# Cosine attention and a two-layer network: 112 or 128 weight columns in the attention's matmuls

## The chip, the cores and the metric

The kernel runs on one core of one Trainium2 chip. The metric is the device time in microseconds of one execution, from the first to the last instruction of the core and what lies around it. The core has an engine for matrix products (TensorE; in the profile PE for matmuls and PEld for the loads of their weights), VectorE (DVE), ScalarE (ACT), GpSimd (POOL), and SyncE (SP), which here only issues transfers. Each engine works through its own queue in order, and waits for the others by semaphores.

## The reference

Eight batches of 12 heads, each with 448 positions of 64 numbers. Queries and keys are brought to length one, the scores are divided by tau = 0.1, and a softmax over the keys weights the values:

```python
q_n = q / (np.linalg.norm(q, axis=-1, keepdims=True) + 1e-06)
k_n = k / (np.linalg.norm(k, axis=-1, keepdims=True) + 1e-06)
scores = np.matmul(q_n, k_n.transpose(0, 1, 3, 2)) / tau
attn = softmax(scores)                 # over the keys
attn_out = np.matmul(attn, v)          # (8, 12, 448, 64)
x = attn_out.transpose(0, 2, 1, 3).reshape(3584, 768)
h = x @ w_in                           # 768 -> 2048
out = (h / (1 + np.exp(-1.702 * h))) @ w_out   # 2048 -> 768
```

Inputs and output are FP32.

## The kernel before

**Tiles.** A unit of attention work is a pair of heads, called x (0 to 47; six to a batch). Its 448 positions are cut into C = 4 chunks of P = 112, which lie on 112 partitions. One load each brings q, k and v of a pair (`load`, L226). Squares and their sums give the norms (`square`, `reduce`, `norm_a`, `norm_b`; `root` and `inverse` for batch 0), `scale` (L310) writes normalised q and k in FP16 into the tile qks, with query (index 0) before key (index 1). For batches 0 and 1 the tile is transposed on TensorE (`transposes`, L333) and copied by DVE (`transposed`, L348), for the later ones by a DMA (`dma_transposed`, L352). Either way qkT holds, on 128 partitions, 64 numbers of the one head over 64 of the other, and along the free axis 448 query positions and 448 key positions.

**Scores.** For a chunk c of keys the 112 key columns are the weights, and the queries move: two matmuls, one for each head, each on 64 of the array's rows. `scores` (L363) takes all 448 queries, for batches 2 to 7; `scores_h` (L424) takes half of them, 224, and two chunks at once, for batches 0 and 1. The result sp has key positions on its partitions. `exp` (L375) makes one of the eight tiles et from it; such a tile has 2 × 448 columns and 64 more, which hold ones from the start (L770).

**Products with values.** The weights are columns of et, that is, query positions; 65 columns move: 64 of the values and a column of ones, which gives the softmax's denominator. `attend` (L388, batches 2 to 7) goes through the queries in four blocks of 128 columns, of which the last runs past the head's 448. `attend_h` (L440, batches 0 and 1, one half of the queries at a time) takes two blocks of 112 for each head, and sums over the four chunks of keys: 16 matmuls. `normalise` or `normalise_h` divides; the result is transposed by a DMA (`turn`, L414) or on TensorE (`turn_h`, L467), into xT.

**The network.** `mm1` (L490; `mm1_h` for batch 0, by halves) multiplies xT with w_in, `tanh` and `gate` apply the activation, `mm2` (L544) multiplies with w_out, `halve` and `store` bring the result out. The weights w_in and w_out are loaded in two halves each by POOL's queue (L582 and L588).

**Order.** The order of the work on every engine is fixed when the program is built. `Plan` (L35) holds every step with its engine, a price in us, a due time, the steps it follows (`after`), and the buffers that it takes and frees. `order` (L71) plays the steps through with those prices; whenever an engine is free, it takes the ready step with the earliest due time. For each change between matmuls on 64 and on 128 rows the price is 0.12 us. `emit` (L48) then emits the steps in that order; before a TensorE step that stands later than TensorE was free, for planned times up to 50 us, it puts fillers (`fill`, L345: a transpose of the identity into an unused part of PSUM). Steps of POOL and DVE that share a port are linked (`port`), so that a POOL step of that kind follows the last such DVE step in the planned order. Some loads are held until others have landed (`hold`): batch 1's loads for w_in, w_out for the last q load of batch 1 (L762), batch 2's first load and with it SP's queue behind it for the second half of w_out (L614).

Of the kernel before, what the change touches and what calls it, by code (L numbers as in the profile page):

```python
# [10 lines left out]
FP32 = mybir.dt.float32  # L11
# [23 lines left out]
class Plan:  # L35
# [6 lines left out]
    def add(self, name, eng, us, due, emit, after=(), takes=(), frees=(), dma=None, rows=128, hold=(), turn=False):  # L42
        after = list(after) + list(hold)
        if turn:
            self.turns.append((due, len(self.turns), name))
        self.ops[name] = (eng, us, due, emit, after, takes, frees, dma, rows, hold)
# [106 lines left out]
def kernel(  # L153
# [12 lines left out]
    B, H, S, D = q.shape  # L166
    NTOK, DM = out.shape
    DFF = moe_w_in.shape[1]
    P = 112
# [10 lines left out]
    SH = S // 2  # L180
# [26 lines left out]
    ps_s = psum("ps_s", 2)  # L207
# [16 lines left out]
    q32, k32, v32, sqs, n2s, nrms, rss, qkss, qkTs = [{} for _ in range(9)]  # L224
# [85 lines left out]
    def scale(x, ti, eng):  # L310
        if x not in qkss:
            qkss[x] = p_qks.tile([P, 2, C, 2, D], FP16, name="qks")
        src = (q32, k32)[ti].pop(x)
        return eng.tensor_tensor(  # L314
            out=qkss[x][:, ti].rearrange("p c j d -> p j c d"),
            in0=src,
            in1=rss[x][:, ti, :, :, None].to_broadcast((P, 2, C, D)),
            op=ALU.mult,
        )


    def values(x, c, e0, e1):
        return vts[x % NV][:, c].rearrange("p j e -> p (j e)")[:, e0:e1]
# [9 lines left out]
    def transposes(x):  # L333
        tps = tps0[:, : 2 * S].rearrange("p (t s) -> p t s", t=2)
        qks = qkss.pop(x)
        for ti in (1, 0):
            for c in range(C):
                nc.tensor.transpose(
                    out=tps[:, ti, c * P : (c + 1) * P],
                    in_=qks[:, ti, c].rearrange("p j d -> p (j d)"),  # L340
                    identity=ident[:P, :P],
                )
        tpss[x] = tps
# [16 lines left out]

    tpss, exps, sps, avps, xss = [{} for _ in range(5)]

    def scores(x, c):  # L363
        qkT = qkTs[x]
        sp = sps[x, c] = ps_s.tile([P, 2, 512], FP32, name="sp")
        for j in range(2):
            nc.tensor.matmul(  # L367
                out=sp[:, j, :S],
                lhsT=qkT[64 * j : 64 * (j + 1), 1, c * P : (c + 1) * P],
                rhs=qkT[64 * j : 64 * (j + 1), 0, :],  # L370
                start=True,
                stop=True,
            )

    def exp(*key):  # L375
        e = exps[key] = ets[len(exps) % NE]
        kw = dict(bias=ebias[:P]) if shift > 0 else {}
        nc.scalar.activation(  # L378
            out=e[:, : 2 * S].rearrange("p (j s) -> p j s", j=2),
            in_=sps.pop(key)[:, :, :S],  # L380
            func=AF.Exp,
            scale=inv_tau,
            **kw,
        )
# [37 lines left out]


    def scores_h(x, h, u):  # L424
        qkT = qkTs[x]
        sp = sps[x, h, u] = ps_s.tile([P, 2, 512], FP32, name="sp")
        for i in range(2):
            c = 2 * u + i
            for j in range(2):
                nc.tensor.matmul(  # L430
                    out=sp[:, j, i * SH : (i + 1) * SH],
                    lhsT=qkT[64 * j : 64 * (j + 1), 1, c * P : (c + 1) * P],
                    rhs=qkT[64 * j : 64 * (j + 1), 0, h * SH : (h + 1) * SH],
                    start=True,
                    stop=True,
                )
# [3 lines left out]
    def attend_h(x, h):  # L440
        ps = avps[x, h] = ps_m.tile([128, 512], FP32, name="mm")
        for i in range(2):
            for j in range(2):
                o = 132 * i + 65 * j
                for c in range(C):
                    at = j * S + (c % 2) * SH + i * P
                    nc.tensor.matmul(  # L447
                        out=ps[:P, o : o + D + 1],
                        lhsT=exps[x, h, c // 2][:, at : at + P],
                        rhs=values(x, c, D * j, D * j + D + 1),  # L450
                        start=(c == 0),
                        stop=(c == C - 1),
                    )
# [146 lines left out]
    add = plan.add  # L600
# [7 lines left out]
    def due_of(x):  # L608
        return x if x < HP else 2 * x

    for x in range(NPAIR):
        s, grp, first = due_of(x), group_of[x], x < HP
        early = due_of(grp[0]) - (4 if first else 8)
        hold = [("w_in", int(x >= HP + 3))] if HP <= x < 2 * HP else [("w_out", 1)] if x == 2 * HP else []  # L614
        for ti, nm in ((1, "k"), (0, "q")):
            add(("load", nm, x), "ACT" if x + ti == 0 else "SP", 0.5, s - 13, partial(load, x, (q32, k32)[ti], (q, k)[ti], nm + "32"),
                takes=[(nm, 1)], dma=PAIR, hold=hold, turn=True)
            pl = sq_pool(x, ti)
            add(("sq", ti, x), "POOL" if pl else "ACT", 1.0 if pl else 0.53, early + ti * 0.1, partial(square, x, ti),
                after=[("load", nm, x)], takes=[("sq", 1), ("port", int(pl))], frees=[("port", int(pl))])  # L620
            add(("red", ti, x), "DVE", 0.6, early + 0.2, partial(reduce, x, ti),
                after=[("sq", ti, x)], frees=[("sq", 1)])
            dve = x == 0 and ti == 0
            add(("scale", ti, x), "DVE" if dve else "POOL", 0.7 if dve else 1.0, early + 0.5 if first else s - 5 - ti * 0.1,
                partial(scale, x, ti, nc.vector if dve else nc.gpsimd),
                after=[("norm", 1, grp)], takes=[("qks", 1), ("port", 1)], frees=[(nm, 1), ("port", 1)])
# [6 lines left out]
        if x == grp[0] and not first:  # L633
# [6 lines left out]
            after=[("load", "v", x)], takes=[("vt", 1), ("port", 1 - ca)], frees=[("v", 1), ("port", 1 - ca)])  # L640
        if x < TURN:
            add(("tp", x), "PE", 0.4, s - 3, partial(transposes, x),
                after=[("scale", 0, x), ("scale", 1, x)], takes=[("a", 1), ("qkT", 1)], frees=[("qks", 2)])
            add(("qkT", x), "DVE", 0.6, s - 3, partial(transposed, x), after=[("tp", x)], frees=[("a", 1)])
        else:
            add(("qkT", x), "SP", 1.3, s - 3, partial(dma_transposed, x),
                after=[("scale", 0, x), ("scale", 1, x)], takes=[("qkT", 1)], frees=[("qks", 2)],
                dma=packets(2 * P, C * D * 4))
        if x < HALF:
            for h in range(2):  # L650
                sh = x + HP * h if first else s + h
                for u in range(2):
                    key = (x, h, u)
                    add(("s",) + key, "PE", 0.2, sh, partial(scores_h, *key), after=[("qkT", x)] + [("s", min(x + AHEAD, HP - 1), 0, 1)] * (first and h),
                        takes=[("sp", 1)], frees=[("qkT", h * u)], rows=64)
                    add(("exp",) + key, "ACT", 0.82, sh + 0.1, partial(exp, *key), after=[("s",) + key],
                        takes=[("exp", 1)], frees=[("sp", 1)])
                es = [("exp", x, h, u) for u in range(2)] + [("cast", x)]
                add(("at", x, h), "PE", 0.85, sh + 1, partial(attend_h, x, h), after=es,
                    takes=[("mm", 1)], frees=[("exp", 2), ("vt", h)])  # L660
                add(("nx", x, h), "DVE", 0.65, sh + 1, partial(normalise_h, x, h), after=[("at", x, h)],
                    takes=[("xs", 1)])
                add(("turn", x, h), "PE", 0.15, sh + 1, partial(turn_h, x, h), after=[("nx", x, h)],
                    frees=[("xs", 1)])
                add(("x", x, h), "ACT" if x in XA and not h else "DVE", 0.35, sh + 1, partial(turned_h, x, h), after=[("turn", x, h)],
                    takes=[("x", 1 - h)], frees=[("mm", 1)])
            continue
        for c in range(C):
            add(("s", x, c), "PE", 0.19, s + c // 2, partial(scores, x, c), after=[("qkT", x)],
                takes=[("sp", 1)], frees=[("qkT", int(c == C - 1))], rows=64)  # L670
            add(("exp", x, c), "ACT", 0.82, s + c // 2 + 0.1, partial(exp, x, c),
                after=[("s", x, c)], takes=[("exp", 1)], frees=[("sp", 1)])
        for j in range(2):
            es = [("exp", x, c) for c in range(C)] + [("cast", x)]
# [19 lines left out]
    for b in range(B):  # L694
# [3 lines left out]
        for u in units:  # L698
            key = u if b else u + ("h",)
            m, half = u[1], not b  # L700
            after = [prev] if prev else []
# [13 lines left out]
        for t in tiles:  # L715
            for n in range(2):
                for part in range(4):
                    if b:
                        after = [("g", b, 4 * part + 3)]
                    else:  # L720
                        after = [("g", h, 4 * part + 2, "h") for h in range(1 + (t > 0))]
# [92 lines left out]
```

## Time and profile before

| | us |
|---|---|
| median of five runs | 452.43 |
| lowest, highest | 450.85, 455.28 |
| the profiled execution | 454.32 |
| its span, first to last instruction | 452.4 |
| PE busy in it | 437.4 |
| ACT busy | 302.7 |
| DVE busy | 239.5 |
| POOL busy | 146.2 |
| matmuls of `attend_h` (L447), busy | 23.7 |
| matmuls of `scores` (L367), `scores_h` (L430), busy | 43.8, 16.7 |

The mean granted clock of TensorE in that execution was 0.995 of full speed. Busy times are sums over the whole span. Matmuls are pipelined, so a line's busy time contains some of its neighbours'; the distance from one start to the next tells what an instruction costs. In the profile a form like 112*128 is the weights' rows and columns, and what follows it is the moving operand. A row of the timeline gives the start, the length, the engine, the line, the operation, output and inputs, shapes and the number of instructions that were put together; in brackets stands the engine's idle time before them and what ended it. A row of the chain gives start, length, and what the time went to; "issue" is time in which the profile shows no wait.

### The profile page before, as it was taken

The page shows a single profiled execution, that of the slowest core. Times are in us where ns is not written, and L with a number is a line of the kernel's source. Part 1 is how long each engine was busy: PE and PEld are TensorE (multiplying, and loading weights), DVE is VectorE, ACT ScalarE, POOL GpSimd, SP SyncE. Part 2 cuts the span into 40 slices and gives each one's busy share as a digit, 9 for nine tenths or more (in the row PEclk, how much of TensorE's full clock was granted, in tenths as well). Part 3 has the DMA queues.
Part 4 walks back from the last instruction along what each step waited for, and adds up shares of the span by engine and source line. Part 5 has one row for each costly group of instructions (what it writes and reads, how often), then busy time and mean ns, then how long its engine had stood idle before and what let it go on. Part 6 is the DMA issues. An engine that isn't in the chain of part 4 may idle for free.

```text
span 452.4 us, 10559 instructions
## 1 busy us (share of the span) xinstructions
PE 437.4 (97%) x4170; PEld 276.1 (61%) x4170; DVE 239.5 (53%) x629; ACT 302.7 (67%) x478; POOL 146.2 (32%) x209
## 2 busy tenths in 40 slices
PE   8899999989989989999999999999999999999996
PEld 8778988655545655556555665566555665555563
DVE  5857986776777736673575427561452115503400
ACT  5878566959989768876787668775776557324421
POOL 2837593176660750625061603433110000000000
PEclk9999999999989999999999999999999999999999
DMA  8999298999996897647653674645301321021022
GB/s 216 243 226 263 52 166 174 253 245 296 249 220 181 153 223 179 124 117 199 166 148 103 168 213 132 148 95 142 80 12 25 83 62 45 12 71 35 1 70 72
DMA packets 95889, 64.00 MB, mean 141 GB/s; under 512 B 56288, under 2 KB 90848, under 8 KB 95840
## 3 DMA queue, kind: packets, MB, share of 16 engines
q1 hardware_dynamic: 91952, 56.81, 52.2%
q0 software_dynamic: 3648, 6.29, 7.7%
q8 instruction: 33, 0.54, 0.5%
q10 hardware_dynamic: 240, 0.23, 0.2%
q14 instruction: 16, 0.13, 0.1%
HBM read 45.61 MB, written 11.01 MB: 125 GB/s over the span
## 4 chain that ended last, share of the span: by engine, by line
PE 64%; DMA 17%; DVE 6%; ACT 4%; SPq 4%; issue 3%; POOL 1%; ACTq 0%; POOLq 0%; DVEq 0%
PE mm L493 22%; PE mm L548 21%; DMA k<-in_k_dram 10%; PE avp L393 6%; PE sp L367 5%; DMA w_out<-in_moe_w_out_dram 4%; PE tps L346 4%; PE mm L447 2%; ACT sq L242 2%; DMA q<-in_q_dram 2%; SPq L229 2%; DMA v<-in_v_dram 2%; ACT et L378 1%; DVE n L248 1%; PE sp L430 1%
## 5 line engine op out<-in xcount | busy, mean ns | idle before, releaser
L378 ACT ACTIVATE et<-sp 112x896 f16<-112x896 f32 x192 | 166.7, 916 | 38.6 <-PE sp L367 27.3
L548 PE MATMUL mm<-w_out,gT 128*128 128x384 f16 x896 | 153.7, 326 | 0.8 <-DVE xT L480 0.8
L493 PE MATMUL mm<-xT,w_in 128*128 128x448 f16 x672 | 135.9, 355 | 0.6 <-DVE gT L510 0.6
L548 PEld LDWEIGHTS <-gT 128*128 128x128 f16 x896 | 84.3, 98 | 65.3 <-issue 12.8
L493 PEld LDWEIGHTS <-w_in 128*128 128x128 f16 x672 | 62.6, 98 | 67.6 <-issue 14.4
L510 DVE SCALAR_TENSOR_TENSOR gT<-th,mm 128x448 f16<-128x448 f16 x112 | 68.4, 616 | 57.3 <-ACT th L503 57.1
L503 ACT ACTIVATE th<-mm 128x448 f16<-128x448 f32 x128 | 69.5, 548 | 34.0 <-PE mm L493 25.5
L248 DVE TENSOR_REDUCE n<-sq 112x8 f32<-112x512 f32 x96 | 64.3, 681 | 49.1 <-ACT sq L242 46.2
L330 POOL CAST vt<-v 112x256 f16<-112x256 f32 x92 | 35.0, 401 | 120.1 <-PE avp L393 87.0
L314 POOL TENSOR_TENSOR qks<-k,y 112x512 f16<-112x512 f32 x42 | 43.8, 1042 | 44.2 <-DVE y L289 25.6
L559 ACT ACTIVATE ost<-mm 128x384 f32<-128x384 f32 x56 | 27.5, 491 | 42.7 <-PE mm L548 40.9
L393 PEld LDWEIGHTS <-et 112*128 112x128 f16 x1152 | 44.8, 98 | 15.7 <-ACT et L378 2.3
L393 PE MATMUL avp<-vt,et 112*128 112x65 f16 x1152 | 47.6, 193 | 3.6 <-ACT et L378 1.9
L314 POOL TENSOR_TENSOR qks<-q,y 112x512 f16<-112x512 f32 x42 | 43.8, 1042 | 3.2 <-DVE y L289 3.2
L404 DVE RECIPROCAL rcx<-avp 128x4 f32<-128x4 f32 x72 | 12.9, 179 | 59.5 <-PE avp L393 59.5
L367 PE MATMUL sp<-qkT 64*112 64x448 f16 x288 | 43.8, 376 | 0.0
L242 ACT ACTIVATE sq<-k 112x512 f32<-112x512 f32 x42 | 26.1, 630 | 24.8 <-DMA k<-in_k_dram 21.9
L407 DVE TENSOR_TENSOR xf<-avp,rcx 128x256 f16<-128x256 f32 x72 | 30.6, 425 | 2.5
L242 ACT ACTIVATE sq<-q 112x512 f32<-112x512 f32 x42 | 26.6, 632 | 3.9 <-DMA q<-in_q_dram 3.7
L447 PE MATMUL mm<-vt,et 112*112 112x65 f16 x384 | 23.7, 217 | 0.9 <-DVE xT L480 0.8
L447 PEld LDWEIGHTS <-et 112*112 112x112 f16 x384 | 22.0, 132 | 2.6 <-issue 2.0
L523 PE MATMUL mm<-xT,w_in 128*128 128x224 f16 x192 | 21.0, 259 | 0.1
(44 smaller groups left out, 226.1 us busy)
## 6 DMA issues: line engine op xcount, KB each, us to landing
k<-in_k_dram SPq DMA_DIRECT2D x48, 224.0 KB, 4.4
v<-in_v_dram SPq DMA_DIRECT2D x48, 224.0 KB, 3.9
q<-in_q_dram SPq DMA_DIRECT2D x47, 224.0 KB, 4.5
w_in<-in_moe_w_in_dram POOLq DMA_DIRECT2D x2, 1536.0 KB, 16.7
w_out<-in_moe_w_out_dram POOLq DMA_DIRECT2D x2, 1536.0 KB, 14.4
out_dram<-ost SPq DMA_DIRECT2D x7, 336.0 KB, 3.0
out_dram<-ost SPq DMA_DIRECT2D x8, 288.0 KB, 2.9
out_dram<-ost SPq DMA_DIRECT2D x8, 240.0 KB, 3.0
```

The source lines that it names most:

```text
L242: return nc.scalar.activation(out=sqs[x, ti], in_=src, func=AF.Square)
L248: nc.vector.tensor_reduce(out=n2s[grp][:, x - grp[0], ti], in_=sqs.pop((x, ti)), axis=AX.X, op=ALU.add,)
L314: return eng.tensor_tensor(out=qkss[x][:, ti].rearrange("p c j d -> p j c d"), in0=src, in1=rss[x][:, ti, :, :, None].to_broadcast((P, 2, ...
L330: copy(out=vt[:, :, j, :D], in_=src[:, j]) for j in range(2)
L367: nc.tensor.matmul(out=sp[:, j, :S], lhsT=qkT[64 * j : 64 * (j + 1), 1, c * P : (c + 1) * P], rhs=qkT[64 * j : 64 * (j + 1), 0, :], start= ...
L378: nc.scalar.activation(out=e[:, : 2 * S].rearrange("p (j s) -> p j s", j=2), in_=sps.pop(key)[:, :, :S], func=AF.Exp, scale=inv_tau, **kw,)
L393: nc.tensor.matmul(out=ps[:, (D + 1) * t : (D + 1) * (t + 1)], lhsT=exps[x, c][:, q0 : q0 + 128], rhs=values(x, c, D * j, D * j + D + 1), ...
L447: nc.tensor.matmul(out=ps[:P, o : o + D + 1], lhsT=exps[x, h, c // 2][:, at : at + P], rhs=values(x, c, D * j, D * j + D + 1), start=(c == 0),
L493: nc.tensor.matmul(out=ps[:, :S], lhsT=w_in_sb[:, kk, 128 * m : 128 * (m + 1)], rhs=xTs[b, kk][:, :S], start=(kk == 0), stop=(kk == KT1 - 1),)
L503: nc.scalar.activation(out=ths[key], in_=mms[key][:, :S], func=AF.Tanh, scale=0.851)
L510: nc.vector.scalar_tensor_tensor(out=gts[b // 2][:, m, (b % 2) * S : (b % 2 + 1) * S], in0=ths.pop((b, m)), scalar=1.0, in1=mms.pop((b, m) ...
L548: nc.tensor.matmul(out=mms[b2, t, n][:, :NW], lhsT=gts[b2][:, kk, 128 * t : 128 * (t + 1)], rhs=w_out_sb[:, kk, NW * n : NW * (n + 1)], st ...
```

## The change

The weights of the score matmuls and of the value products of batches 0 and 1 become 128 columns wide. A chunk still begins at a multiple of 112, and its last 16 columns are the first 16 of what follows: of the next chunk of keys, or, after the last one, of the queries; for that, keys now stand before queries in qks and in qkT. In et the last block runs into the columns of ones. The tile sp and the written part of the value product's PSUM have 128 partitions instead of 112; `exp` and `normalise_h` read the first 112 of them, as before. The planner's price of an `attend_h` goes from 0.85 to 0.48 us; with it the planned order changes on all engines.

```diff
@@ scale
-            out=qkss[x][:, ti].rearrange("p c j d -> p j c d"),
+            out=qkss[x][:, 1 - ti].rearrange("p c j d -> p j c d"),
@@ transposes
-                    out=tps[:, ti, c * P : (c + 1) * P],
-                    in_=qks[:, ti, c].rearrange("p j d -> p (j d)"),
+                    out=tps[:, 1 - ti, c * P : (c + 1) * P],
+                    in_=qks[:, 1 - ti, c].rearrange("p j d -> p (j d)"),
@@ new
+    def keys(x, j, c):
+        kT = qkTs[x].rearrange("p t s -> p (t s)")
+        return kT[64 * j : 64 * (j + 1), c * P : c * P + 128]
+
+    def queries(x, j, s0, s1):
+        return qkTs[x][64 * j : 64 * (j + 1), 1, s0:s1]
@@ scores
-        sp = sps[x, c] = ps_s.tile([P, 2, 512], FP32, name="sp")
+        sp = sps[x, c] = ps_s.tile([128, 2, 512], FP32, name="sp")
-                lhsT=qkT[64 * j : 64 * (j + 1), 1, c * P : (c + 1) * P],
-                rhs=qkT[64 * j : 64 * (j + 1), 0, :],
+                lhsT=keys(x, j, c),
+                rhs=queries(x, j, 0, S),
@@ exp
-            in_=sps.pop(key)[:, :, :S],
+            in_=sps.pop(key)[:P, :, :S],
@@ scores_h
-        sp = sps[x, h, u] = ps_s.tile([P, 2, 512], FP32, name="sp")
+        sp = sps[x, h, u] = ps_s.tile([128, 2, 512], FP32, name="sp")
-                    lhsT=qkT[64 * j : 64 * (j + 1), 1, c * P : (c + 1) * P],
-                    rhs=qkT[64 * j : 64 * (j + 1), 0, h * SH : (h + 1) * SH],
+                    lhsT=keys(x, j, c),
+                    rhs=queries(x, j, h * SH, (h + 1) * SH),
@@ attend_h
-                        out=ps[:P, o : o + D + 1],
-                        lhsT=exps[x, h, c // 2][:, at : at + P],
+                        out=ps[:, o : o + D + 1],
+                        lhsT=exps[x, h, c // 2][:, at : at + 128],
@@ the plan
-                add(("at", x, h), "PE", 0.85, sh + 1, partial(attend_h, x, h), after=es,
+                add(("at", x, h), "PE", 0.48, sh + 1, partial(attend_h, x, h), after=es,
```

More of the change, by code (lines that the diff above doesn't have):

```diff
@@ L361 @@
     tpss, exps, sps, avps, xss = [{} for _ in range(5)]
+    def keys(x, j, c):
[3 more added lines that the diff above has]
+        return qkTs[x][64 * j : 64 * (j + 1), 1, s0:s1]
     def scores(x, c):
-        qkT = qkTs[x]
-        sp = sps[x, c] = ps_s.tile([P, 2, 512], FP32, name="sp")
+        sp = sps[x, c] = ps_s.tile([128, 2, 512], FP32, name="sp")
         for j in range(2):
@@ L424, in scores_h @@
     def scores_h(x, h, u):
-        qkT = qkTs[x]
-        sp = sps[x, h, u] = ps_s.tile([P, 2, 512], FP32, name="sp")
+        sp = sps[x, h, u] = ps_s.tile([128, 2, 512], FP32, name="sp")
         for i in range(2):
```

## The prediction

> **What bounds the kernel now.** I read the page's busy shares and chain first, then the groups by shape, then PE's timeline stretch by stretch. The page:
>
> ```profile
> PE 437.4 (97%) x4170; PEld 276.1 (61%) x4170; DVE 239.5 (53%) x629; ACT 302.7 (67%) x478; POOL 146.2 (32%) x209
> PE 64%; DMA 17%; DVE 6%; ACT 4%; SPq 4%; issue 3%; POOL 1%; ACTq 0%; POOLq 0%; DVEq 0%
> PE   8899999989989989999999999999999999999996
> ACT  5878566959989768876787668775776557324421
> ```
>
> PE is the engine to watch, but the 97% hides two stages. Before 50 us PE's busy time contains fillers (L346, 250 transposes of the identity: 14 us at 56 ns from start to start). From 50 to 101 us, where batch 2's scores (L367) begin, the chain runs through weights and loads, not through PE:
>
> ```profile
> 51.94 0.41 PE tps L338 x8
> 52.37 0.62 DVE qkT L350
> 53.00 0.53 DVE gT L535
> ...
> 55.87 0.20 DVE y L289
> 56.07 0.29 issue
> 56.36 0.53 POOL w_out L590
> ...
> 57.30 18.09 DMA w_out<-in_moe_w_out_dram
> 75.41 0.03 issue
> 75.44 0.31 SPq L229
> ```
>
> From the chain of waits: POOL issues w_out only when DVE has ended a norm, which stands in DVE's queue behind a copy of PE's transposes; all loads of batch 2 stand in SP's queue behind w_out's landing. From 131 us on PE follows itself without a gap.
>
> Next, what one matmul really takes. Its recorded end says little, so I take start to next start, in PE's timeline (start, length, engine, line; two stretches):
>
> ```profile
> 41.87 0.59 PE L430 MATMUL sp<-qkT 64*112 64x224 f16 x8
> 42.40 1.32 PE L523 MATMUL mm<-xT,w_in 128*128 128x224 f16 x12
> ...
> 49.72 0.97 PE L447 MATMUL mm<-vt,et 112*112 112x65 f16 x16
> 50.52 0.45 PE L523 MATMUL mm<-xT,w_in 128*128 128x224 f16 x3
> ...
> 384.36 0.65 PE L393 MATMUL avp<-vt,et 112*128 112x65 f16 x16
> 384.85 2.43 PE L493 MATMUL mm<-xT,w_in 128*128 128x448 f16 x12
> ```
>
> Sixteen products with values take 0.80 us with 112 weight columns (L447) and 0.49 us with 128 (L393), both with 65 moving columns: 50 against 30 ns each. Only the weights differ, so L447 is paced by its weight loads. The loads' own records agree: 132 ns at 112x112, 98 ns at 112x128.
>
> **What the Trainium skill says.** "TensorE: Matmul & The Clock Gate", section "Weight-path perf modes — Fast Weight Load (FWL) and DoubleRow", says that the fast load is on when the number of weights is 128 and the type is not FP32. The pair 50 and 30 ns above agrees for loads over 112 rows; no row here shows it for 64 rows. Same page, "What overlaps and what doesn't": a load runs ahead of matmuls in flight only where its row group differs. The trace agrees in part: 128-row loads of L493 are hidden under 128-row matmuls (189 ns apart), but every change between 64 and 128 rows costs time. Same page, "What's actually happening": an idle window halves PE's clock. Here, after two waits, six L493 matmuls from 128.85 us took 2.09 us instead of 1.14. "Perfetto Trace Analysis", "Tensor Engine Instruction (MATMUL, LD_WEIGHTS)": PE's end times are estimates, hence the starts.
>
> **The change part by part.**
>
> (a) Values of batches 0 and 1: 24 groups (12 head pairs, 2 halves) of 16 matmuls go from 112 to 128 weight columns. Each saves 0.80 − 0.49 = 0.31 to 0.32 us: 7.7 us of PE. The sixteen extra output rows are written and never read. New waits: none, since one exp writes all that the wider load reads, but for the 64 columns of ones that are set at the start.
>
> (b) Scores, all batches. Two pairs take 0.52 us (375.92 to 376.44), one pair 0.33 (104.11 to 104.44): a pair adds 0.19, which is its 448 moving columns (6 of L493 with 448 take 1.14). So 0.14 us of each visit is not streaming, and entering from 128 rows costs 0.09 more (L393 to L367 0.58, to L493 0.49): 0.23 us a visit. Of this the records show one weight load: in the visit at 375.92 the second pair's loads start 47 to 48 ns after the first's, and its matmuls 234 ns after the first's, 47 more than streaming. That part should shrink to what a 128-column load leaves uncovered: the first L493 matmul after a visit is followed 200 ns later instead of 189, so 11 ns; at most 30, L393's pitch. Saving 17 to 36, I take 30 ns. Inside a visit loads are covered by streaming (97 ns a pair for L430, 189 for L367), so nothing more. The program has 108 visits (74 to L367's, 34 to L430's): 3.2 us. Were the fast load refused for 64 rows, 128 columns at the old pace cost 47 × 16/112 = 7 ns a visit, 0.8 us lost.
>
> (c) The layout: keys before queries in qks and qkT. Same tiles, same counts of transposes, copies and DMAs, one write for each tile; no time.
>
> (d) The planner's price of a value group, 0.85 to 0.48 us, rewrites the fixed order on every engine. Counted in both orders: visits to scores fall from 77 to 74 (L367) and 35 to 34 (L430), 4 × 0.23 = 0.9 us saved; fillers rise from 250 to 288, 38 × 0.056 = 2.1 us added, in the first 60 us; 92 instead of 84 second-layer matmuls (L548) stand before batch 2's first scores, so 8 × 0.163 = 1.3 us moves forward.
>
> Sum on PE: 7.7 + 3.2 + 0.9 − 2.1 = 9.7 us. Up to batch 2's first scores it is 7.7 + 1.0 + 0.2 − 2.1 − 1.3 = 5.5; after them 2.2 + 0.7 + 1.3 = 4.2.
>
> What of the first 5.5 is on the path? There DMA sets the pace, so w_out's issue decides. POOL's timeline before:
>
> ```profile
> 48.80 1.04 POOL L241 TENSOR_TENSOR sq<-q 112x512 f32<-112x512 f32 x1 [2.96 <-DVE y L289]
> 49.80 1.04 POOL L314 TENSOR_TENSOR qks<-k,y 112x512 f16<-112x512 f32 x1
> ...
> 56.36 1.82 POOL L590 DMA_DIRECT2D w_out<-in_moe_w_out_dram  x2 [2.52 <-DVE y L289]
> ```
>
> The first norm of batch 1 ends at 48.7, five POOL steps follow, then 2.5 us waiting for the second norm. In the new order six steps of 1.0 us follow the first norm, and the first half of w_out waits only for the last q load of batch 1 (landed 48.1); the wait for the second norm stands before the second half, which has some 10 us of cover, since the first half takes 10.8 us to land. So with the norm where it was, w_out starts at 48.7 + 6.1 = 54.8, 1.5 us earlier. The norm itself follows the eleventh value group; PE gets there 11 × 0.32 − 0.7 (13 more fillers) + 0.3 (visits) = 3.1 us earlier if nothing else holds it, 0 if the squares do. Gain 1.5 to 4.7; I take 3.5, and PE (5.5 ahead) is then in time. Behind the second half's wait on POOL stand batch 1's scalings, which the transposes need; they wait for that norm anyway. What is late next is batch 2's loads on SP, at 101 to 127 us.
>
> After the first scores PE is full, so 4.2 us should arrive; I take off 0.7 for longer waits at 101 to 131, where ACT is busy 28.1 of 30 us. Total 3.5 + 4.2 − 0.7 = 7.0. The profiled execution took 454.3 (span 452.4): 447.3. It lies 1.9 above the median of five, 452.4, so the median should come to 445.4.
>
> **The rivals.**
>
> All of it: the 9.7 us reach the end, 442.7. For it: PE is 97% busy. Against: loads set the pace before 101 us.
>
> Hidden early: w_out starts no earlier, because DVE's queue or POOL's squares hold the norm, and only the visits after 101 us count, 2.9 us: 449.5. For it: that stretch of the chain is DMA. Against: the new order takes the second norm from before the first half.
>
> Not what it says: the fast load needs more than 128 columns (chunks start at multiples of 112 elements, where L393 starts at multiples of 64), and 128 slow columns cost 57 instead of 50 ns: 24 × 16 × 7 = 2.7 us plus 0.8 plus 2.1 of fillers, less 0.9: 457. Nothing in the profile speaks for it.
>
> Slower, by waits at batch 2's start. PE's timeline there:
>
> ```profile
> 124.63 0.64 PE L393 MATMUL avp<-vt,et 112*128 112x65 f16 x16 [0.65 <-DVE xf L407]
> 126.98 0.95 PE L393 MATMUL avp<-vt,et 112*128 112x65 f16 x16 [0.97 <-DVE xf L407]
> 128.78 2.15 PE L493 MATMUL mm<-xT,w_in 128*128 128x448 f16 x6
> ```
>
> Counted from starts, those two waits cost 0.7 + 1.3 us, and the halved clock after them 1.55 (126.98 to 130.87 against 2.34): an episode of 3.5 us. No fillers are planned past 50 us. In the new order two visits there have six score matmuls, so PE asks ACT for more exps at once. If the early gain is hidden and more such episodes come, one cancels the remaining 2.9 us; three give 452.4 − 2.9 + 10.5 = 460. It decides from one on.
>
> **How the numbers follow.** About 1% (4.5 us) is what a measurement of this kernel tells from no change. Forecast 445.4: 0.44. All of it 442.7: 0.19. Hidden early 449.5: 0.20. No fast load 457: 0.05. Slower 460: 0.12. Faster by over 1% (under 447.9): 0.19 + 0.41 + 0.04 = 0.64. Slower (over 457): 0.11 + 0.02 = 0.13. The rest, 0.23, is the same. The range goes from 441.5, just under the whole sum, to 456, between the hidden case and the slow ones.
>
> **What would show it.** Right: sixteen value products of batches 0 and 1 in 0.49 us from start to start, their loads near 98 ns; a visit of two pairs 0.49 instead of 0.52; w_out issued near 53 us; batch 2's first scores near 97.5. Wrong: w_out's first half still at 56; score loads of 64 rows with a second pair still 234 ns after the first; new waits of PE over 0.5 us with a clock below 1 between 90 and 140 us.

## The result

The changed kernel takes 449.6 us (median of 27 runs) against 453.1 for the kernel before (46 runs): a ratio of 0.991 with a 95% interval of 0.990 to 0.993. By the ratio that is 3.9 us less, by the two medians 3.5. That is faster beyond its interval, but by less than the 1% that the prediction took as its bound. The forecast was 7.0 us less; the range held the time.

The profile that was recorded first came from an execution whose matmul clock stood at 0.85 from end to end; what follows is read from two later profiled executions of the changed kernel, "again" and "again2", with clocks of 0.990 and 0.996. They took 451.5 and 446.6 us. At full clock, executions of this kernel lie between 445.4 and 453.7, so a single profile is compared here by its stages and not by its end.

The page of the changed kernel, in again2 (busy time, share of the span, instructions):

```profile
PE 428.1 (96%) x4208; PEld 264.3 (59%) x4208; DVE 236.3 (53%) x629; ACT 301.1 (68%) x478; POOL 146.2 (33%) x209
```

PE's busy time fell by 9.3 us from 437.4, although 38 fillers were added. The groups by shape show where, for the weight loads of the kernel before and for the changed one (again):

```profile
L447 PEld LDWEIGHTS <-et 112*112 112x112 f16 x384 | 22.0, 132 | 2.6 <-issue 2.0 <-ACT et L378 0.3
L367 PEld LDWEIGHTS <-qkT 64*112 64x112 f16 x288 | 13.4, 125 | 6.8 <-issue 3.1
...
L454 PE MATMUL mm<-vt,et 112*128 112x65 f16 x384 | 16.1, 193 | 0.5 <-ACT ost L566 0.3 <-ACT et L386 0.2
L454 PEld LDWEIGHTS <-et 112*128 112x128 f16 x384 | 14.0, 97 | 2.6 <-issue 1.5 <-ACT et L386 0.3 <-DVE gT L542 0.2
L375 PEld LDWEIGHTS <-qkT 64*128 64x128 f16 x288 | 8.9, 94 | 8.7 <-issue 4.9
```

Lines have moved by seven or eight: L454 is the matmul of `attend_h` (L447 before), L401 that of `attend`, L375 that of `scores`, L437 that of `scores_h`. The weight loads of the value products went from 132 to 97 ns a record, those of the scores, over 64 rows, from 125 to 94. What matters is the distance from start to start, in PE's timeline (a visit to the scores in the kernel before, then again):

```profile
375.92 0.59 PE L367 MATMUL sp<-qkT 64*112 64x448 f16 x4
376.44 3.58 PE L493 MATMUL mm<-xT,w_in 128*128 128x448 f16 x18
...
48.48 0.65 PE L454 MATMUL mm<-vt,et 112*128 112x65 f16 x16
48.97 2.46 PE L530 MATMUL mm<-xT,w_in 128*128 128x224 f16 x24
...
360.53 0.55 PE L375 MATMUL sp<-qkT 64*128 64x448 f16 x4
361.01 0.66 PE L555 MATMUL mm<-w_out,gT 128*128 128x384 f16 x3
```

Sixteen value products now take 0.49 us instead of 0.80. A visit to the scores of two pairs takes 0.485 instead of 0.518 (from the records' starts). In the records, the second pair's weight loads start 15 ns after the first pair's instead of 48 (from the first load of each), and its matmuls 200 ns after the first's instead of 234. Streaming alone takes 189 ns, so 11 ns stay uncovered where 45 did.

The load of w_out, in POOL's timeline of again:

```profile
51.52 1.04 POOL L314 TENSOR_TENSOR qks<-k,y 112x512 f16<-112x512 f32 x1
52.52 1.04 POOL L314 TENSOR_TENSOR qks<-q,y 112x512 f16<-112x512 f32 x1
53.51 0.94 POOL L597 DMA_DIRECT2D w_out<-in_moe_w_out_dram  x1
56.10 0.87 POOL L597 DMA_DIRECT2D w_out<-in_moe_w_out_dram  x1 [1.65 <-DVE y L289]
```

Its first half starts at 53.5 instead of 56.4 us, right behind the scalings; only the second half waits for DVE's norm. It lands at 72.4 instead of 75.4, and SP issues batch 2's first load at once. The profile's chain through that stretch, though, no longer passes through w_out (again):

```profile
67.74 0.20 DVE y L289
...
73.43 1.39 POOL vt L330 x4
74.83 6.60 DMA v<-in_v_dram
81.45 7.08 DMA q<-in_q_dram
```

It passes through the scalings and casts of batch 1 on POOL; a cast makes the buffer of a v load free, here 2.5 us after w_out has landed, and in again2 the chain takes the same way. So in the changed kernel two things let batch 2's loads go at nearly the same time. Batch 2's first scores start at 97.5 us (95.3 in again2) instead of 101.1 (100.9 in a second profile of the kernel before). So both times of the early part came as forecast, or sooner. What did not come is the rest, and PE's timeline of again2 after those first scores shows where it went:

```profile
106.75 0.36 PE L375 MATMUL sp<-qkT 64*128 64x448 f16 x2 [0.82 <-ACT et L386]
...
121.57 0.64 PE L401 MATMUL avp<-vt,et 112*128 112x65 f16 x16 [0.19 <-DVE y L261]
122.15 0.36 PE L375 MATMUL sp<-qkT 64*128 64x448 f16 x2
123.12 0.36 PE L375 MATMUL sp<-qkT 64*128 64x448 f16 x2 [0.61 <-ACT et L386]
123.93 0.42 PE L375 MATMUL sp<-qkT 64*128 64x448 f16 x2 [0.44 <-ACT et L386]
124.52 2.40 PE L500 MATMUL mm<-xT,w_in 128*128 128x448 f16 x6 [0.16 <-DVE gT L517]
```

The first row and the three from 122.15 on belong to the two visits of six score matmuls that the new order holds. Each needs three buffers of scores and there are two, so PE waits for ACT to read one; ACT's timeline at the second visit:

```profile
120.03 1.80 ACT L386 ACTIVATE et<-sp 112x896 f16<-112x896 f32 x2
121.73 0.54 ACT L510 ACTIVATE th<-mm 128x448 f16<-128x448 f32 x1
122.15 1.73 ACT L386 ACTIVATE et<-sp 112x896 f16<-112x896 f32 x2
123.74 1.00 ACT L510 ACTIVATE th<-mm 128x448 f16<-128x448 f32 x2
```

ACT goes from exp to tanh to exp without a gap. After PE's waits its clock is halved (for 3.4 us from 124.1), and six L500 matmuls take 2.2 us instead of 1.14.

To put sums to this I give each group of matmuls its pace from start to start (0.189 us for L500, 0.163 for L555, 0.030 for L401, 0.050 or 0.030 for a value product of batches 0 and 1 with 112 or 128 columns, 0.14 or 0.107 besides streaming for a visit to the scores and 0.09 before it); whatever a group takes beyond that, halved clock included, is counted as waiting. The last group, 128 second-layer matmuls that take 20.6 us in every one of these executions, stands in no column. Per profiled execution, in us:

| kernel | first scores of batch 2 | PE work before them | fillers | waits before | PE work after | waits after |
|---|---|---|---|---|---|---|
| before, two profiles | 101.1, 100.9 | 75.6 | 14.3 | 9.9, 9.7 | 318.1 | 7.9, 7.7 |
| changed, again and again2 | 97.5, 95.3 | 67.7 | 16.6 | 11.9, 9.6 | 313.6 | 12.9, 10.3 |
| all widths, old price and order | 100.6 | 66.8 | 14.3 | 18.2 | 315.5 | 6.1 |
| value products alone, old order | 103.4 | 68.0 | 14.3 | 19.8 | 318.1 | 5.5 |
| scores alone, old order | 100.3 | 74.4 | 14.3 | 10.3 | 315.5 | 8.7 |
| new price alone, 112 columns | 103.0 | 76.5 | 16.6 | 8.6 | 316.1 | 10.8 |
| all widths, old order, w_out untied | 97.2 | 66.8 | 14.3 | 14.7 | 315.5 | 7.8 |
| 112 columns, old order, w_out untied | 99.7 | 75.6 | 14.3 | 8.5 | 318.1 | 6.1 |

### The profile page after: what moved, and what is told of

Its sections match the earlier page's. It is cut to its first block, busy times and chain, and to the rows that moved or that the text cites. A ratio compares the mean times of both kernels' runs of the same rounds, so it can differ in the third digit from the quotient of the medians.

```text
span 490.1 us, 10624 instructions
## 1 busy us (share of the span) xinstructions
PE 477.9 (98%) x4208; PEld 282.9 (58%) x4208; DVE 238.4 (49%) x629; ACT 306.1 (62%) x478; POOL 146.6 (30%) x209
## 4 chain that ended last, share of the span: by engine, by line
PE 95%; DVE 2%; ACT 2%; issue 1%; POOL 0%; POOLq 0%; ACTq 0%
PE mm L555 35%; PE mm L500 31%; PE avp L401 8%; PE sp L375 7%; PE tps L346 4%; PE mm L530 4%; PE mm L454 3%; PE sp L437 2%; PE tps L338 1%; ACT et L386 1%; DVE qkT L350 1%; PE mm L477 0%; DVE n L248 0%; DVE gT L517 0%; ACT ost L566 0%
## 5 line engine op out<-in xcount | busy, mean ns | idle before, releaser
L555 PE MATMUL mm<-w_out,gT 128*128 128x384 f16 x896 | 175.2, 357 | 0.5 <-ACT ost L566 0.5
L500 PE MATMUL mm<-xT,w_in 128*128 128x448 f16 x672 | 155.2, 391 | 0.1
L555 PEld LDWEIGHTS <-gT 128*128 128x128 f16 x896 | 91.0, 105 | 80.2 <-issue 14.4
L500 PEld LDWEIGHTS <-w_in 128*128 128x128 f16 x672 | 67.7, 105 | 80.3 <-issue 15.0
L401 PEld LDWEIGHTS <-et 112*128 112x128 f16 x1152 | 47.8, 100 | 15.7 <-PE sp L375 1.2
L401 PE MATMUL avp<-vt,et 112*128 112x65 f16 x1152 | 50.3, 199 | 0.5 <-DVE xf L415 0.5
L375 PE MATMUL sp<-qkT 64*128 64x448 f16 x288 | 42.9, 370 | 2.1 <-ACT et L386 1.2
L242 ACT ACTIVATE sq<-k 112x512 f32<-112x512 f32 x42 | 26.3, 628 | 10.9 <-DMA k<-in_k_dram 10.6
L242 ACT ACTIVATE sq<-q 112x512 f32<-112x512 f32 x42 | 26.3, 629 | 2.1 <-DMA q<-in_q_dram 1.1
L346 PE MATMUL tps<-ident 128*128 128x128 f16 x288 | 22.0, 241 | 3.8 <-DVE qkT L350 2.5
L530 PE MATMUL mm<-xT,w_in 128*128 128x224 f16 x192 | 23.1, 279 | 0.0
L346 PEld LDWEIGHTS <-ident 128*128 128x128 f16 x288 | 19.8, 109 | 5.5 <-issue 4.1
```

The costliest lines, as they stand in the source:

```text
L242: return nc.scalar.activation(out=sqs[x, ti], in_=src, func=AF.Square)
L346: nc.tensor.transpose(out=tps0[:, 2 * S : 2 * S + 128], in_=ident, identity=ident)
L375: nc.tensor.matmul(out=sp[:, j, :S], lhsT=keys(x, j, c), rhs=queries(x, j, 0, S), start=True, stop=True,)
L401: nc.tensor.matmul(out=ps[:, (D + 1) * t : (D + 1) * (t + 1)], lhsT=exps[x, c][:, q0 : q0 + 128], rhs=values(x, c, D * j, D * j + D + 1), ...
L500: nc.tensor.matmul(out=ps[:, :S], lhsT=w_in_sb[:, kk, 128 * m : 128 * (m + 1)], rhs=xTs[b, kk][:, :S], start=(kk == 0), stop=(kk == KT1 - 1),)
L530: nc.tensor.matmul(out=ps[:, i * SH : (i + 1) * SH], lhsT=w_in_sb[:, kk, 128 * (m + i) : 128 * (m + i + 1)], rhs=xTs[0, kk][:, h * SH : (h ...
```

## The experiments

All times are medians, with the ratio to the kernel before on the same chip and its 95% interval. Three chips served: one for the first four experiments, one for the value products alone, w_out untied with all widths and the two mixed prices, and one for the other four.

**The change again**, for its profile.

> The changed kernel again, for a profile at full clock. Theory 1 (the step that was too large is the early one: w_out starts some 2.5 us sooner, but less of that reaches batch 2's first scores): 3.5 to 4.5 us under the kernel before, first scores of batch 2 at 99 to 101 us instead of 101.1, a visit of two pairs in 0.49 us. Theory 2 (the gain before the first scores arrives, and waits between 101 and 131 us take it back): first scores at 97 to 98 us, and 3 to 4 us more idle time of PE after them than before. Theory 3 (score loads over 64 rows stay slow): second pair 234 ns after the first, nothing saved after 101 us.

448.8 against 453.7 us, 0.988 (0.983 to 0.992). First scores at 97.5, a visit at 0.485 us: theory 3 falls. Work after the first scores is 4.5 us less, and waits after them are 5.0 us more. Theory 2 holds for this execution, but not in its place: between 101 and 131 us the waits are 2.1 us more, the rest of the 5.0 lies later. Theory 1, that the early gain doesn't arrive, does not hold.

**All widths, with the old price**, and with it the old order on every engine.

```diff
-                add(("at", x, h), "PE", 0.48, sh + 1, partial(attend_h, x, h), after=es,
+                add(("at", x, h), "PE", 0.85, sh + 1, partial(attend_h, x, h), after=es,
```

> All widths of the change, but the planner's old price of 0.85 us for a value group, so that every engine has its old order and PE its old 250 fillers. Theory 1: w_out is still behind the second norm, which comes 2 to 3 us sooner with PE; first scores at 98.5 to 100, then 77 visits x 0.03 = 2.3 us: 3.5 to 5 us under the kernel before, as good as the change itself. Theory 2: the new order's waits are gone, so 6 us or more under before. If the new order is what brings the gain: 0 to 2 us under before.

449.9 against 453.7 us, 0.990 (0.985 to 0.994), 3.8 us under. That lies in theory 1's span, but not for its reason: first scores came at 100.6 and not before 100. PE has 8.8 us less to do before them and waits 8.3 us longer. After them waits fell to 6.1. So much the same gain comes by another way: little of it early, nearly all of it late.

**The new price alone**, in the kernel before.

```diff
-                add(("at", x, h), "PE", 0.85, sh + 1, partial(attend_h, x, h), after=es,
+                add(("at", x, h), "PE", 0.48, sh + 1, partial(attend_h, x, h), after=es,
```

> The kernel before, 112 columns everywhere, with the new price of 0.48 us alone: the new order and its 288 fillers. Theory 1: 2.1 us of fillers are added, PE falls behind a plan that takes its groups for short, w_out starts sooner all the same: 0 to 2.5 us over the kernel before. Theory 2: the new order's waits cost 3 to 4 us, so 3 us or more over before. If the order is what brings the gain: 2 us or more under before.

455.0 against 453.7 us, 1.003 (1.001 to 1.004): slower, by 1.3 us, as theory 1 had it. The 2.3 us of fillers are there, and 2.9 us more waits after the first scores. The new order is worse where value groups are slow, though it has fewer visits. This run also separates widths and order: at 97 to 140 us its waits are 6.0, as with all widths in the new order (6.1 and 6.2), while the seven profiled executions in the old order, narrow and wide, have 2.3 to 4.1. So these waits belong to the order, whatever the widths. With all widths the new order made no difference in time that can be told from the old one (0.988 against 0.990, six runs each).

**The scores alone** at 128 columns.

```diff
-                        out=ps[:, o : o + D + 1],
-                        lhsT=exps[x, h, c // 2][:, at : at + 128],
+                        out=ps[:P, o : o + D + 1],
+                        lhsT=exps[x, h, c // 2][:, at : at + P],
```

(with the old price)

> The scores' weights at 128 columns, the value products of batches 0 and 1 at 112 as before, old price and old order. Theories 1 and 2: 77 visits after 101 us save 0.03 us each, 2.3 us, and the 35 before it at most 1.1: 2.3 to 3.4 us under the kernel before. Theory 3: no gain, 0 to 1 us over before.

451.7 against 453.7 us, 0.995 (0.993 to 0.998): 2.0 us less, a little below the expected 2.3 to 3.4, which lies within the interval. PE's work fell by 1.2 us before the first scores and 2.6 after them.

**The value products alone** at 128 columns.

```diff
-                lhsT=keys(x, j, c),
+                lhsT=keys(x, j, c)[:, :P],
```

(in `scores` and `scores_h`, their tiles at 112 partitions, the old price)

> Only the value products of batches 0 and 1 at 128 columns, scores at 112, old price and old order. PE saves 24 x 0.32 = 7.7 us, all of it before batch 2's first scores. If loads pace that stretch: first scores 0 to 1 us sooner than 101.1 us, the rest turns into waits of PE between 50 and 97 us, 0.5 to 2 us under the kernel before in all. If PE paced it: 5 us or more under before.

452.5 against 453.1 us, 0.998 (0.996 to 1.000): no difference that can be told, and 1.9 us at most. PE's work before the first scores fell by 7.6 us, its waits rose by 9.9 in the profiled execution, which started w_out late, at 58.5. PE doesn't pace the stretch up to batch 2; this is the largest saving of the change, and by itself little or nothing of it arrives. The waits are now ones that weren't there before, in PE's timeline of this run:

```profile
65.44 1.31 PE L530 MATMUL mm<-xT,w_in 128*128 128x224 f16 x12 [0.37 <-DVE xT L487]
69.13 0.27 PE L477 MATMUL mm<-ident,xs 112*128 112x112 f16 x2 [0.24 <-DVE xs L467]
86.69 0.64 PE L454 MATMUL mm<-vt,et 112*128 112x65 f16 x14 [2.05 <-ACT et L386]
```

**All widths, old order, w_out not tied to the norm.** The planner's order stays to the instruction; only the link from DVE's last norm to w_out's two loads goes.

```diff
-                elif port is not None:
+                elif port is not None and names[i][0] != "w_out":
```

(with the old price)

> All widths with the old price and order, and w_out's two loads no longer tied to the second norm on DVE: they follow POOL's scalings at once. If w_out's landing paces what comes after: w_out is issued near 53 instead of 55.5 us, batch 2's first scores come 2 to 2.5 us sooner than with all widths in the old order (100.6), and the time is 2 to 2.5 us under that kernel's, 6 us under the kernel before. If something else paces that stretch: no change against all widths in the old order.

POOL's timeline of this run:

```profile
52.26 1.04 POOL L314 TENSOR_TENSOR qks<-q,y 112x512 f16<-112x512 f32 x1
53.25 1.82 POOL L597 DMA_DIRECT2D w_out<-in_moe_w_out_dram  x2
55.78 1.04 POOL L314 TENSOR_TENSOR qks<-k,y 112x512 f16<-112x512 f32 x1 [0.71 <-DVE y L289]
```

w_out starts at 53.2 instead of 55.5, the first scores at 97.2 instead of 100.6, with PE's work the same and 3.5 us less waiting before them. That w_out paces the first scores in this order is shown, and the other runs agree: in 12 of the 13 profiled executions at full clock the first scores come 23.9 to 26.3 us after w_out's second half has landed, while the landing itself lies anywhere from 68.6 to 77.6 us. The exception is the new price alone, 28.5 us. The time was 447.7 against 453.1 us, 0.990 (0.986 to 0.994); the ratio is that of the widths in the old order, 0.990, and the intervals of 0.8 points leave open how much of the 3.4 us reaches the end.

**The same in the kernel before**, 112 columns everywhere.

> The kernel before, 112 columns and the old order, with w_out's two loads alone no longer tied to the second norm on DVE. It shows whether the load's start paced the kernel before, or only one with wide weights. If loads paced batch 2's first scores: w_out near 53.9 instead of 56.4 us, first scores 1.5 to 2.5 us sooner than 101.1, 1 to 2.5 us under the kernel before. If PE has no room left with 112 columns: 1 us under at most.

452.3 against 453.0 us, 0.998 (0.996 to 1.000), 0.7 us less. w_out at 54.3, first scores at 99.7, 1.1 to 1.4 sooner. That is what was expected if PE has little room with 112 columns: only 8.5 us of waits are left before the first scores, against 14.7 with 128. It fits a kernel before in which two things held the first scores at nearly the same time, PE's narrow weights and w_out's wait: taking one away alone moved them by 0.3 to 1.4 us (widths alone, w_out alone), both by 3.7 to 3.9. The small steps are of the size by which two executions of one kernel differ, so this is likely and not shown: w_out started 1.3 us later in the second profile of the kernel before than in the first, and the first scores came 0.2 us sooner.

**w_out sooner still.**

```diff
-        add(("w_out", i), "POOL", 1.0, 9 + i, partial(load_w_out, i), hold=[("load", "q", 2 * HP - 1)],
+        add(("w_out", i), "POOL", 1.0, 5 + i, partial(load_w_out, i), hold=[("load", "q", 2 * HP - 1)],
```

(on top of the untied w_out, with all widths)

> All widths, old price, w_out not tied to the norm, and w_out's due time 5 instead of 9, so that POOL issues it after the first of the four scalings; the planner's order changes from there on (32 instead of 84 second-layer matmuls before batch 2's first scores). If the load's start still paces: w_out near 50 us, first scores 2 to 4 us sooner than with w_out after the scalings (97.2), 0 to 3 us under that kernel. If PE's work before the first scores paces by now, or the new order brings waits as the changed kernel's did: no gain, or up to 4 us over it.

451.2 against 453.0 us, 0.997 (0.994 to 0.999). w_out at 49.5, first scores at 92.5, but the order changed as well: only 57.9 us of PE's work lies before them, 324.8 after, and waits before them rose to 18.9. By the ratios it is slower than with w_out behind the scalings. The first scores are a marker only while the same work stands before them.

**The new price for batch 0 alone, and for batch 1 alone.**

```diff
-                add(("at", x, h), "PE", 0.85, sh + 1, partial(attend_h, x, h), after=es,
+                add(("at", x, h), "PE", 0.48 if first else 0.85, sh + 1, partial(attend_h, x, h), after=es,
```

> All widths, the new price for batch 0 alone, the old one for batch 1: the early order with w_out's first half ahead of the second norm, 288 fillers, but another order after 97 us, with one visit of six score matmuls instead of two. If the order after batch 2's first scores takes the gain back in the changed kernel: first scores at 97 to 98.5 us, less waiting after them than the changed kernel's 6.2 us at 97 to 140, and 1 to 3 us under the changed kernel. If it does not: within 1 us of the changed kernel.

452.0 against 453.1 us, 0.997 (0.995 to 0.999). Waits of 4.7 us at 97 to 140, fewer than the changed kernel's, as expected. First scores at 94.7, sooner than the expected 97 to 98.5; but only 72 second-layer matmuls stand before them instead of 92, so that they don't compare. And it is slower than the changed kernel, not faster; the expectation failed. Its profiled execution, 449.4 us, was the fastest of its 22, so the profile doesn't show what the others lose.

> All widths, the old price for batch 0, the new one for batch 1 alone: the old early order (250 fillers, w_out behind the second norm), and a new order of batch 1 and after, with one visit of six score matmuls. If w_out's start sets batch 2's first scores: 100 to 101 us. If the later order takes the gain back: waits of 5 us or more at 97 to 140, and 1 to 3 us over all widths in the old order.

(the two prices exchanged) 452.4 against 453.1 us, 0.998 (0.996 to 1.000). First scores at 100.5, where the old early order puts them, and 5.9 us of waits at 97 to 140, both as expected; 2.4 us over all widths in the old order by the medians, 3.9 by the ratios. Here too the profiled execution, 449.4, was the fastest of 22. That the later order costs something agrees with this; how much is not to be read from it.

**Both kernels once more**, for their waits.

> The changed kernel in another profiled execution, to see which of its waits come back. If the waits are the order's: 5 to 7 us of waits at 97 to 140 us again, and first scores at 97 to 98.5. If they are of one execution: 4 us or less.

446.6 us. Waits at 97 to 140 us: 6.1, after 6.2 in the first profile, and in the same places: 0.77 before an `attend`, 1.22 at the first visit of six, 0.58, then 1.7 at the second visit of six and some 1.5 at half clock. They are the order's. First scores came at 95.3, sooner than the expected 97 to 98.5; w_out started 2.0 us sooner than in the first profile. Two things in this list qualify the picture. The wait before the `attend` is for a cast or a scaling of POOL (0.70 us idle in both profiles), not for ACT. And the kernel before has an episode of waits and half clock at 123 to 131 us too, which the second visit of six replaces; what the new order adds is chiefly the first visit and the wait for POOL.

> The kernel before in another profiled execution, for the same reason. If the waits are the order's: about 4 us of waits at 97 to 140 us again, first scores at 100.5 to 101.5; if they are of one execution: 6 us or more, or 2 or less.

454.0 us. Waits at 97 to 140 us: 4.0, after 4.1, again where they were. What differs between the two profiles of the changed kernel lies later: at 240 to 300 us the first has 4.0 us of waits, with a second halved clock at 273 us, and again2 has 1.5.

## Why the prediction was right in sign and too large

**(a) Value products: right.** 24 groups went from 0.80 to 0.49 us; the fast load works at starts that are multiples of 112 elements, so the "not what it says" case is out. Value products alone cut PE's work by 7.6 us where 7.7 was forecast.

**(b) Visits to the scores: right, a little under-sized.** 0.033 us a visit instead of 0.030; the load that stays uncovered is 11 ns, the lower end of the bound. (The 47 ns that the prediction starts from are 45 by its own pace of 189 ns: 234 less 189.) Where the prediction says that the trace "agrees in part" with loads that run ahead only where the row group differs, its own lines have two sides: the hidden loads of L493 are over the same 128 rows as the matmuls that hide them (189 ns apart), which speaks against it; what agrees is that a change of rows costs some 0.09 us. Loads over 64 rows are fast too, which no row of the kernel before could show. On their own they gained 2.0 us, near the 2.3 that lie after the first scores: this part lies where PE paces, and it reaches the end.

**(c) The layout** left no trace of its own: counts of instructions and transfers for q and k are what they were. No run has the new layout without wide weights of one kind or the other.

**(d) The new order.** Fillers cost 2.3 us more (2.1 forecast), the visits and the eight matmuls moved forward are as counted. With (a) and (b), PE's work and fillers before the first scores fell by 5.6 us (5.5 forecast), after them by 4.5 (4.2 forecast).

**The early gain: right, or under-sized.** 3.5 was taken from bounds of 1.5 to 4.7; w_out started 2.9 to 6.1 us sooner and the first scores 3.4 to 5.8, from the pairs of profiles. The place in POOL's queue is worth what was worked out: from POOL's first step behind the first norm to w_out it is 6.0 us in both profiles of the changed kernel and 7.6 in both of the kernel before, 1.6 less where 1.5 was forecast. The rest, 1.3 to 4.5 us, is that step coming sooner (47.5 and 45.6 against 48.8 and 50.1), where the forecast had 0 to 3.1. How much of it PE's saving brought stays open: the step lies at 47.9 with all widths in the old order, but at 50.9 with the value products alone. The chain behind it is as told up to the loads, w_out and then what waits for it; but POOL's casts, which the prediction didn't count there, let the loads go at nearly the same time. The "hidden early" case was the fate of the widths alone, not of the changed kernel: the new price put w_out's first half ahead of the second norm, and with that the early saving came through, as it did where w_out was untied.

**The step that failed is "I take off 0.7 for longer waits at 101 to 131".** Its mechanism was named, in the rival with waits at batch 2's start: visits of six score matmuls ask ACT for more exps than it has made. No working stands behind its size. Measured from the first scores to the end, waits grew by 2.4 to 5.2 us: 2.1 of them at 97 to 140 us in both executions, the rest later and different between the two. In that sum 3.5 + 4.2 − 0.7 the last term should have been 2.4 to 5.2, which gives 2.5 to 5.3 us; measured over many runs: 3.9. The agreement is not to be pressed. Against the profiles before, the two profiled executions of the changed kernel are 2.5 to 2.9 and 7.4 to 7.7 us shorter. The second meets the forecast of 7.0, but by two errors that cancel: an early gain of 5.6 to 5.8 us and 2.4 to 2.6 us of waits. How the 3.9 of the median divides is not shown. The warning was in the prediction itself: ACT was busy 28.1 of 30 us in that stretch, which leaves little room for an order that brings PE there sooner and asks for three tiles of scores where two fit. One such visit cost 1.2 us of waits, the other 1.7 and a halved clock, in place of a like episode before; the rival's three more episodes of 3.5 us each were too many, and the forecast's 0.7 too little. The sign that the prediction had named for it is there too: waits of PE over 0.5 us with a clock below 1 between 90 and 140 us; but it tells little, since the kernel before has such an episode as well.

What stays open: why executions of the same kernel lie over 4 to 8 us, and why the price of batch 0 alone or batch 1 alone gives 452 us when their profiled executions, the fastest of each, took 449.4. A profile of an ordinary execution of those was not taken. A third buffer for scores, which might take the waits of the six-matmul visits away, was not tried.

No version was found that is shown to beat the changed kernel: all widths with w_out untied has the lower median, 447.7, but at 0.990 (0.986 to 0.994) it can't be told from 0.991 (0.990 to 0.993).

## What to carry to other kernels

A saving on the busiest engine is worth what the stage where it falls lets through: here 7.6 us in a stage that loads paced were worth under 2 us alone, and 2.6 us in a stage that PE paced (with 1.2 before it) were worth 2.0. When two things seem to hold a stage at nearly the same time, here narrow weights and a load behind a norm, change them together as well as one by one. And a price in a planner is a change of its own: it moves every queue, so look in the new order for places that ask an engine which is already full for more at once, and cost them one by one.

## What the runs showed of the hardware

Weight loads of 128 FP16 columns were fast over 64 rows as well as over 112, and at starts that are multiples of 112 elements; between two pairs of score matmuls 11 ns of one stay uncovered (200 less 189), against 45 for 112 columns (234 less 189). Sixteen more columns of weights made a matmul with 65 moving columns cheaper, 30 instead of 50 ns. What the wider weights don't touch is the change between 64 and 128 rows itself: about 0.09 us on the way in (0.122 to 0.125 us from the last `attend` matmul to the scores, against its pace of 0.030) and as much on the way out (0.28 us from the last scores to the next L500, against 0.189) stayed the same with both widths.
